# A retention layer that feeds a two-product block: another PSUM order in the dense product, stores on SyncE's queue, input scalings spread over a block, another opening

## The chip, the core and the metric

The kernel runs on one core of a Trainium2 chip. A core has a matrix engine (TensorE, PE in the profile), a vector engine (VectorE, DVE), a scalar engine (ScalarE, ACT), a general engine (GpSimd, POOL) and an engine that mostly issues transfers (SyncE, SP). Each works through its own list of instructions in order, and waits on semaphores. PE writes to PSUM, which the kernel uses as eight banks, each as large as a 128 x 512 tile of float32; DVE and ACT read PSUM and write SBUF. Transfers between memory and SBUF are done by 16 DMA engines, which take their work from queues; a queue belongs to the engine that issues to it. The metric is device time in microseconds (us) of one execution.

## What is computed

```python
def _attn_ref(q, k, v):                    # each (4, 8, 768, 64)
    gamma = 1.0 - 2.0 ** (-5.0 - np.arange(H))
    for t in range(S):
        state = gamma[None, :, None, None] * state + np.einsum('bhd,bhe->bhde', k[:, :, t], v[:, :, t])
        y[:, :, t] = scale * np.einsum('bhd,bhde->bhe', q[:, :, t], state)

def _moe_ref(x, w_in, w_out, alpha):       # x (3072, 512), w_in (512, 2048), w_out (2048, 512)
    h = x @ w_in
    g = np.maximum(h, 0.0) + alpha * np.minimum(h, 0.0)
    return g @ w_out
```

`x` is `y` with its heads side by side: 4 x 768 = 3072 tokens of 8 x 64 = 512 values. Inputs and output are float32 in memory; the products run in float16 and sum in float32.

## The kernel before

**Visits.** The retention is cut into 24 visits `w` of 256 time steps and 4 heads. A visit needs `load(w)`, three transfers of 256 KB (`ks`, `qs`, `vs`), all issued on SP's queue; `prep(w)`, which scales k and q by powers of gamma into one float16 tile `kdq` (k on DVE for the first eight visits and on POOL later, q on POOL) and converts v to `vx` (ACT for the first eight visits, POOL later); and the transposition of `kdq` into `kq`. For visits 0 to 7 PE does this (`turn(w)`: eight transposes into a PSUM tile `trb`, read by one ACT instruction); from visit 8 on a DMA does, issued on SP's queue in `prep`. Then PE computes the scores within 64 row pairs (`scores`, tile `sc`), the sums for the state (`state_sums`, tiles `st`), and, once DVE has masked the scores into `m2`, the values `y` (`within`, and `finish` with the rest of the `carried` part); ACT copies `y` to `xT`. `visit(w_old, w_new)` runs the end of one visit around the beginning of the next.

**Blocks.** Four visits give a block of 512 tokens, and there are six blocks. `ffn1(n)` computes 16 output tiles of 128 x 512, each as four matmuls; ACT then makes `hm` = relu(-h) and DVE `gt` = h + (1 - alpha) hm, in float16. `ffn2(n)` runs 64 matmuls into four PSUM tiles `ops`; each is copied to `os` by ACT and stored, 256 KB per store, by a transfer that ACT issues. Both are Python generators, one `yield` per matmul; `tick(gen, m)` emits m of them, so that the order of everything is written out by hand. While `ffn2(n)` runs, the visits of block n + 1 are ticked in; while `ffn1(n)` runs, `ahead()` emits `prep(w)` for a visit two blocks or so ahead, with its transposing DMA and the loads of visit w + 4 behind it. Block 0 and the first half of block 1 differ: the opening runs visits 0 to 3 alone, visits 4 to 7 run in and behind `ffn2(0)` (in four parts of 16 products) and in `ffn1_half(1, 0)`.

**PSUM.** Eight banks: tag `f` two single banks, `p` two single banks, `s` one tile of two banks, `y` one tile of two banks. `sc` and `trb` take `s`, `y` takes `y`, `st` takes `p`, `ops` takes `f`. `ffn1` takes its tiles from the class `Banks`, by a string: `f` and `p` ask for a bank, `s` or `y` for a two-bank tile, whose first half it gives out, and a capital letter gives the second half of the tile asked for last.

**DMA semaphores.** Transfers that SP and ACT issue share eight semaphores in turn (`DMAHW0` to `DMAHW7` in the orders below), so the issue of each waits for the transfer eight before it. The loads from visit 4 on are held (`held`) until a part of `w_out` has landed. Buffers: `ks`, `qs`, `vs`, `kdq`, `vx` and `kq` eight each, `os` six, `hm` three, `gt` two.

Among the lines of the profile: L140 loads, L157 scalings, L172 transposing DMA, L177 and L179 `vx`, L192 ACT's copy of `trb`, L213 scores, L270 and L292 `y`, L313 `xT`, L339 `gt`, L350 `hm`, L360 and L381 matmuls of `ffn1` and `ffn1_half`, L405 those of `ffn2`, L414 `os`, L418 the store.

## Time and profile before

| | before |
|---|---|
| median of 3 runs | 306.46 us (304.01 to 307.71) |
| profiled execution | 305.05 us, span of its instructions 303.3 us |
| busy: PE, DVE, ACT, POOL | 215.9, 134.1, 98.6, 57.9 us |
| mean granted clock of PE | 0.927 of full speed |
| chain that ended last | PE 57%, DVE 12%, ACT 9%, DMA 8% |
| output copies `os` and stores | 24 of each, stores on ACT's queue, 256 KB |
| transfers of SP's queue | 72 loads of 256 KB, 16 transposes |

Busy time is that of instructions that work; waiting, and the issuing of transfers, count as idle. An engine's waits are put down to the instruction of another engine, or the DMA, that ended last before the wait did. The chain follows the last instruction back to what released each. A granted clock of 1.0 is 2.4 GHz, 0.5 is 1.2 GHz. The DMA share is the mean busy share of the 16 DMA engines.

### The profile page before, as it was taken

To read this page: it belongs to the slowest core of one execution; us is meant where nothing else is said; L and a number is where in the kernel's file an instruction comes from. 1 tells how busy PE (TensorE), PEld (TensorE's weight loads), DVE (VectorE), ACT (ScalarE), POOL (GpSimd) and SP (SyncE) were. 2 spreads that over 40 slices of the span, in tenths; PEclk is the share of its full clock that TensorE was granted. 3 is DMA by queue.
4 is the path that set the end of the run, shared out by engine and by line. 5 is a ranking of instruction groups with operands and counts; after the bars stand their busy time and mean duration, and the time that the engine had idled before them with its cause. 6 is when DMAs were issued, how large, how long until landed. Compare 5 with 4: busy or idle time off the path is not lost.

```text
span 303.3 us, 5146 instructions
## 1 busy us (share of the span) xinstructions
PE 215.9 (71%) x2145; PEld 109.4 (36%) x2145; DVE 134.1 (44%) x242; ACT 98.6 (33%) x162; POOL 57.9 (19%) x68
## 2 busy tenths in 40 slices
PE   1659669946596877623769996699966999669900
PEld 0543324435484434201224542245422454224400
DVE  1754463433685733004356744655346652461000
ACT  3444341326462021104332353423434224351100
POOL 1740049800135634000006600000000000000000
PEclk9999999975999979775699999999999999999985
DMA  7999999619469999998000998001110011100111
GB/s 233 253 202 199 238 338 336 174 45 89 104 183 243 215 258 173 116 139 229 18 0 17 89 92 72 15 7 45 51 40 0 4 45 52 43 0 2 47 51 41
DMA packets 62599, 34.08 MB, mean 112 GB/s; under 512 B 18400, under 2 KB 59504, under 8 KB 62576
## 3 DMA queue, kind: packets, MB, share of 16 engines
q1 hardware_dynamic: 54912, 23.08, 43.5%
q0 software_dynamic: 4224, 4.19, 8.7%
q10 hardware_dynamic: 3440, 6.48, 5.9%
q8 instruction: 17, 0.28, 0.5%
q14 instruction: 6, 0.05, 0.1%
HBM read 27.45 MB, written 6.29 MB: 111 GB/s over the span
## 4 chain that ended last, share of the span: by engine, by line
PE 57%; DVE 12%; ACT 9%; DMA 8%; SPq 4%; ACTq 2%; issue 2%; POOL 2%; POOLq 0%
PE hps L360 24%; PE ops L405 24%; DVE gt L339 10%; ACT hm L350 5%; DMA kq<-kdq 4%; DMA ks<-in_k_dram 3%; PE sc L213 2%; ACTq L418 2%; PE hps L381 2%; SPq L140 2%; ACT kq L192 2%; DVE m L244 2%; PE y L270 2%; SPq L172 2%; DMA vs<-in_v_dram 1%
## 5 line engine op out<-in xcount | busy, mean ns | idle before, releaser
L339 DVE SCALAR_TENSOR_TENSOR gt<-hm,oma,hps 128x512 f16<-128x512 f32 (+1 forms) x112 | 73.1, 670 | 85.8 <-ACT hm L350 82.7
L360 PE MATMUL hps<-xT,win 128*128 128x512 f16 x320 | 79.8, 403 | 42.1 <-DVE gt L339 39.1
L405 PE MATMUL ops<-wout,gt 128*128 128x512 f16 x384 | 90.3, 385 | 2.4 <-ACT os L414 2.4
L350 ACT ACTIVATE hm<-hps 128x512 f32<-128x512 f32 x96 | 56.8, 597 | 81.2 <-PE hps L360 57.9
L360 PEld LDWEIGHTS <-win 128*128 128x128 f16 x320 | 32.6, 102 | 88.2 <-issue 56.8
L405 PEld LDWEIGHTS <-gt 128*128 128x128 f16 x384 | 35.8, 99 | 44.3 <-issue 4.9
L244 DVE TENSOR_TENSOR m<-sc,mi 128x1024 f16<-128x1024 f32 x24 | 29.4, 1223 | 14.4 <-PE sc L213 12.7
L157 POOL TENSOR_TENSOR kdq<-qs,tab 128x512 f16<-128x512 f32 x24 | 25.7, 1071 | 33.9 <-DMA qs<-in_q_dram 33.8
L313 ACT ACTIVATE xT<-y 128x512 f16<-128x512 f32 x24 | 14.3, 596 | 53.0 <-PE y L270 34.7
L157 POOL TENSOR_TENSOR kdq<-ks,tab 128x512 f16<-128x512 f32 x16 | 16.7, 1042 | 61.4 <-PE st L231 40.3
L414 ACT ACTIVATE os<-ops 128x512 f32<-128x512 f32 x24 | 14.3, 596 | 31.9 <-PE ops L405 30.7
L270 PE MATMUL y<-kq,tg 64*64 64x128 f16 x160 | 13.2, 256 | 11.3 <-ACT xT L313 7.7
L381 PE MATMUL hps<-xT,win 128*128 128x256 f16 x128 | 16.0, 281 | 4.5 <-DVE gt L339 3.3
L301 DVE MEMSET warm<- 1x1 f32 x24 | 1.4, 59 | 32.5 <-PE y L292 32.4
L258 DVE TENSOR_TENSOR tg<-ss,tab 128x128 f16<-128x128 f32 x32 | 14.8, 461 | 1.1
L381 PEld LDWEIGHTS <-win 128*128 128x128 f16 x128 | 12.4, 100 | 7.1 <-DVE gt L339 3.9
L179 POOL CAST vx<-vs 128x512 f16<-128x512 f32 x16 | 10.2, 639 | 22.4 <-PE y L292 11.3
L270 PEld LDWEIGHTS <-tg 64*64 64x64 f16 x160 | 6.3, 111 | 22.2 <-issue 15.4
L187 PE MATMUL trb<-mi,kdq 128*128 128x128 f16 x64 | 7.3, 279 | 9.5 <-DVE kdq L157 4.5
L213 PE MATMUL sc<-kq 64*64 64x128 f16 x384 | 11.3, 241 | 2.6 <-ACT kq L192 2.6
L192 ACT ACTIVATE kq<-trb 128x1024 f16<-128x1024 f16 x8 | 8.2, 1023 | 14.0 <-PE trb L187 13.4
L292 PE MATMUL y<-m,vx 64*64 64x128 f16 x384 | 11.8, 240 | 0.0
(21 smaller groups left out, 68.8 us busy)
## 6 DMA issues: line engine op xcount, KB each, us to landing
ks<-in_k_dram SPq DMA_DIRECT2D x24, 256.0 KB
qs<-in_q_dram SPq DMA_DIRECT2D x24, 256.0 KB
vs<-in_v_dram SPq DMA_DIRECT2D x24, 256.0 KB
out_dram<-os ACTq DMA_DIRECT2D x24, 256.0 KB
win<-in_moe_w_in_dram POOLq DMA_DIRECT2D x4, 512.0 KB, 7.7
wout<-in_moe_w_out_dram POOLq DMA_DIRECT2D x4, 512.0 KB, 15.1
kq<-kdq SPq DMA_TRANSPOSE x16
mi<-mi_const ACTq DMA_DIRECT2D x1, 128.0 KB
```

The source lines that it names most:

```text
L157: eng.tensor_tensor(out=kdq[:, kind].rearrange("p z r d -> p r z d"), in0=src.rearrange("p (r x) (a d) -> p r (x a) d", a=2, x=2), in1=tab ...
L213: nc.tensor.matmul(out=sc[half(c), at : at + 128], lhsT=kq[half(r), 2 * x + a, half(c)], rhs=kq[half(r), 4 + 2 * x : 6 + 2 * x, half(c)], ...
L244: nc.vector.tensor_tensor(out=m2.rearrange("p s a i -> p s (a i)"), in0=sc.rearrange("p (s n) -> p s n", n=256), in1=mask.unsqueeze(1).to_ ...
L258: nc.vector.tensor_tensor(out=tg, in0=stv, in1=decay, op=MULT)
L270: ins = nc.tensor.matmul(out=y[half(x), 512 * c + 128 * r : 512 * c + 128 * r + 128], lhsT=tgs[2 * u + c, g][half(r), x, :], rhs=kq[half(r ...
L313: nc.scalar.activation(out=xT[n][:, 2 * g : 2 * g + 2, TU * i : TU * i + TU].rearrange("p r (c i) -> p c r i", c=2), in_=y.rearrange("p (c ...
L339: nc.vector.scalar_tensor_tensor(out=gt[:, ft, lo:hi], in0=hm, scalar=oma_sb[:, ft : ft + 1], in1=hps, op0=MULT, op1=ADD,)
L350: nc.scalar.activation(out=hm, in_=hps, func=RELU, bias=0.0, scale=-1.0)
L360: nc.tensor.matmul(out=hps, lhsT=w_in_all[:, hp, 128 * ft : 128 * ft + 128], rhs=xT[n][:, hp, :], start=(hp == 0), stop=(hp == NP - 1),)
L381: nc.tensor.matmul(out=hps[:, TU * j : TU * j + TU], lhsT=w_in_all[:, hp, 128 * (f0 + j) : 128 * (f0 + j) + 128], rhs=xT[n][:, hp, lo:hi], ...
L405: nc.tensor.matmul(out=opss[tq], lhsT=gt[:, ft, 128 * tq : 128 * tq + 128], rhs=w_out_all[:, ft, :], start=(ft == 0), stop=(ft == NFT - 1),)
L414: nc.scalar.activation(out=os_sb, in_=opss[tq], func=COPY, bias=0.0, scale=1.0)
```

## The change

`ffn1` takes its tiles in the order `spyfSpYf`, and `Banks` remembers the first halves by tag, so that the second half can be asked for later. The stores are issued on `nc.sync`, SP's queue. In blocks 1 to 5 the four `ahead()` of a block, which were all in `ffn1`, stand two in `ffn1` (after 20 matmuls each) and two in `ffn2`. In the opening the loads come in another order, `turn` writes `trb` to a bank of tag `f` or `p`, products on a tile of ones (`busy`) are put in at four places, the state sums of visits 2 and 3 for the second chunk move into `ffn1(0)`, and visits 4 to 6 run inside an `ffn2(0)` that is in one piece, ahead of which stand the four `prep`. `visit` passes on a list of chunks (`cs`). Cut to its core:

```diff
+    ones = sbp.tile([128, 256], F16, tag="ones", name="ones")[:, 0:128]
-    def ps_s(name, dt=FP):
-        return ps(name, "s", 1024 if dt == FP else 2048, dt, 1)
     class Banks:
-            self.order, self.i, self.pair = order, 0, None
+            self.order, self.i, self.pairs = order, 0, {}
             if at in "sy":
-                self.pair = ps(name, at, 1024, FP, 1)
-                return self.pair[:, 0:512]
-            return self.pair[:, 512:1024]
+                self.pairs[at] = ps(name, at, 1024, FP, 1)
+                return self.pairs[at][:, 0:512]
+            return self.pairs[at.lower()][:, 512:1024]
-    def prep(w, opening=False, between=None):
+    def prep(w, opening=False, k_on=None):
-        scaled(nc.vector if opening else nc.gpsimd, 0, t["k"])
+        scaled(k_on or (nc.vector if opening else nc.gpsimd), 0, t["k"])
-        if between:
-            between()
+    def busy(m):
+        ips = ps("idle", "f")
+        for _ in range(m):
+            nc.tensor.matmul(out=ips[:, 0:128], lhsT=ones, rhs=ones, start=True, stop=True)
-    def turn(w):
+    def turn(w, tag, fill=0):
-        trb = ps_s("trb", F16)
+        trb = ps("trb", tag, 1024, F16)
         for i in range(8):
+            if i == 4 and fill:
+                busy(fill)
-    def ffn1(n, order="ffppsSyY"):
+    def ffn1(n, order="spyfSpYf"):
-                        nc.scalar.dma_start(
+                        nc.sync.dma_start(
+    nc.vector.memset(ones, 1.0)
-    for w in range(3):
-        load(w)
-    load(3, "kqv")
+    for w, which in ((0, "kqv"), (1, "kq"), (2, "kq"), (1, "v"), (3, "kq"), (2, "v"), (3, "v")):
+        load(w, which)
+    busy(34)
     prep(0, opening=True)
-    turn(0)
+    turn(0, "f", 12)
     prep(1, opening=True)
-    visit(None, 0)
+    busy(16)
+    scores(0)
...
+    prep(2, opening=True)
+    get_wi(0)
+    state(0)
...
+    turn(1, "f")
+    within(0)
+    scores(1)
+    state_sums(1)
+    finish(0)
+    masked(1)
+    prep(3, opening=True, k_on=nc.gpsimd)
+    state(1)
...
+    within(3)
+    busy(8)
+    finish(3)
     for w in range(WB, 3 * WB):
         load(w)
-    for _ in ffn1(0):
-        pass
-    gen = ffn2(0, parts=4, order="ffyY")
-    tick(gen, 44)
-    prep(4, opening=True)
-    turn(4)
...
+    gen = ffn1(0)
+    tick(gen, 32)
+    for w in (2, 3):
+        state_sums(w, (1,))
+        state(w, (1,))
     for _ in gen:
         pass
+    gen = ffn2(0)
+    for w in range(WB, 2 * WB):
+        prep(w, opening=True)
+    tick(gen, 30)
+    turn(4, "p")
+    tick(gen, 6)
+    visit(None, 4)
...
     gen = ffn1_half(1, 0, "ffpp")
     tick(gen, 8)
-    turn(7)
+    turn(7, "f")
...
-    gen = ffn1_half(1, 1, "ffppsSyY")
+    gen = ffn1_half(1, 1, "spyfSpYf")
     for n in range(1, NBLK):
         if n > 1:
             gen = ffn1(n)
-            for i in range(WB):
-                tick(gen, 14)
+            for i in range(2):
+                tick(gen, 20)
                 ahead()
...
             for i in range(1, WB):
-                tick(gen, 14)
+                tick(gen, 8)
+                if i == 2:
+                    ahead()
+                tick(gen, 6)
                 visit(w0 + i - 1, w0 + i)
-            tick(gen, 12)
+            tick(gen, 6)
+            ahead()
+            tick(gen, 6)
             within(w0 + WB - 1)
```

What this does to the lists of instructions shows at three places.

PE's list in `ffn1` of block 2, before (the matmuls alone, four for each tile; `hps` is an output tile, one number for both halves of a two-bank tile; a bracket says which engine's semaphore an instruction waits for):

```order
L360 MATMUL hps_1645<-xT2_1403,win_68 128x512
...
L360 MATMUL hps_1666<-xT2_1403,win_68 128x512
...
L360 MATMUL hps_1666<-xT2_1403,win_68 128x512 [waits DVE_49]
...
L360 MATMUL hps_1681<-xT2_1403,win_68 128x512 [waits PE_49]
...
L360 MATMUL hps_1681<-xT2_1403,win_68 128x512 [waits DVE_49]
```

The two halves of `hps_1666` come one right after the other, and the second waits for DVE; so it is with `hps_1681`. The same list after the change, in the same block:

```order
L377 MATMUL hps_1724<-xT2_1480,win_69 128x512 [waits Activation_49]
...
L377 MATMUL hps_1732<-xT2_1480,win_69 128x512
...
L377 MATMUL hps_1740<-xT2_1480,win_69 128x512 [waits PE_49]
...
L377 MATMUL hps_1748<-xT2_1480,win_69 128x512
...
L377 MATMUL hps_1724<-xT2_1480,win_69 128x512 [waits DVE_49]
...
L377 MATMUL hps_1776<-xT2_1480,win_69 128x512
...
L377 MATMUL hps_1740<-xT2_1480,win_69 128x512 [waits DVE_49]
...
L377 MATMUL hps_1791<-xT2_1480,win_69 128x512 [waits Activation_49]
```

Between the halves of `hps_1724` now stand three other tiles, as between those of `hps_1740`; the second half still has a wait for DVE.

SP's list where the transposes for block 3 begin (visits 12 and 13), before; `DMAHW` is one of the eight DMA semaphores:

```order
L172 DMA_TRANSPOSE kq12_1650<-kdq12_1648 128x8x128 [waits DMAHW3_49,PE_49,Pool_49]
L140 DMA ks16_1655<-in_k_dram 128x4x128 [waits DMAHW4_49,DVE_49]
L140 DMA qs16_1657<-in_q_dram 128x4x128 [waits DMAHW5_49]
L140 DMA vs16_1659<-in_v_dram 128x4x128 [waits DMAHW6_49,Activation_49]
L172 DMA_TRANSPOSE kq13_1691<-kdq13_1689 128x8x128 [waits DMAHW7_49,PE_49,Pool_49]
```

And after, at the same place:

```order
L435 DMA out_0_dram<-os_1416 2x64x512 [waits DMAHW3_49,Activation_49]
L171 DMA_TRANSPOSE kq12_1503<-kdq12_1501 128x8x128 [waits DMAHW4_49,PE_49,Pool_49]
L141 DMA ks16_1508<-in_k_dram 128x4x128 [waits DMAHW5_49,DVE_49]
L141 DMA qs16_1510<-in_q_dram 128x4x128 [waits DMAHW6_49]
L141 DMA vs16_1512<-in_v_dram 128x4x128 [waits DMAHW7_49]
L435 DMA out_0_dram<-os_1581 2x64x512 [waits DMAHW0_49,Activation_49]
L435 DMA out_0_dram<-os_1660 2x64x512 [waits DMAHW1_49,Activation_49]
L171 DMA_TRANSPOSE kq13_1668<-kdq13_1666 128x8x128 [waits DMAHW2_49,PE_49,Pool_49]
```

The stores, which ACT issued, stand between the loads and transposes, each with a wait for ACT's copy, and take their turns in the eight semaphores.

ACT's list in the opening, from its first conversion of v on (`vx`), before:

```order
L177 ACTIVATE vx0_100<-vs0_77 128x512 [waits DMAHW5_49]
L192 ACTIVATE kq0_101<-trb_105 128x1024 [waits PE_49]
L177 ACTIVATE vx1_116<-vs1_83 128x512 [waits DMAHW0_49]
L192 ACTIVATE kq1_117<-trb_167 128x1024 [waits PE_49]
L177 ACTIVATE vx2_178<-vs2_89 128x512 [waits DMAHW3_49]
L313 ACTIVATE xT0_241<-y_184 128x2x2x128 [waits PE_49]
L192 ACTIVATE kq2_179<-trb_251 128x1024 [waits PE_49]
```

And after:

```order
L176 ACTIVATE vx0_137<-vs0_79 128x512 [waits DMAHW5_49]
L201 ACTIVATE kq0_138<-trb_142 128x1024 [waits PE_49]
L176 ACTIVATE vx1_166<-vs1_89 128x512 [waits DMAHW2_49]
L176 ACTIVATE vx2_228<-vs2_95 128x512 [waits DMAHW5_49]
L201 ACTIVATE kq1_167<-trb_241 128x1024 [waits PE_49]
L329 ACTIVATE xT0_308<-y_251 128x2x2x128 [waits PE_49]
```

The conversion of v of visit 2 (`vx2`) now stands ahead of the copy of visit 1's transposes (`kq1`).

## Rows read from the trace of the kernel before

**Rows 1.** The page, section 1: busy us (share of the span), count of instructions.

```profile
PE 215.9 (71%) x2145; PEld 109.4 (36%) x2145; DVE 134.1 (44%) x242; ACT 98.6 (33%) x162; POOL 57.9 (19%) x68
```

**Rows 2.** Chain of waits, in order of time: start us, us, engine, what, count.

```profile
23.87 5.90 PE hps L360 x20
...
72.88 1.44 PE hps L381 x6
...
97.29 0.35 PE sc L213 x16
...
159.62 0.35 PE sc L213 x16
...
274.55 13.83 PE ops L405 x64
```

**Rows 3.** Windows: stretch, us, busy PE PEld DVE ACT POOL, PEclk, DMA share, GB/s.

```profile
121.20:159.00 37.80, 19.68 (x65) 7.38 (x64) 10.86 (x15) 9.72 (x17) 0.00 (x0) 0.73 0.64 101
...
177.20:197.50 20.30, 14.31 (x65) 6.17 (x64) 11.10 (x15) 9.48 (x16) 0.00 (x0) 1.00 0.64 53
197.50:215.70 18.20, 18.20 (x267) 9.00 (x266) 8.32 (x19) 4.70 (x9) 0.00 (x0) 1.00 0.09 31
```

**Rows 4.** Waits of PE (us, times, longest), in 177 to 216, then 45 to 97.

```profile
PE hps L360 <- DVE gt L339: 6.0, 4, 1.5
...
PE hps L381 <- DVE gt L339: 3.3, 2, 1.7
```

**Rows 5.** Timeline in a late ffn1: start us, us, engine line op, [idle before <-releaser].

```profile
182.98 1.89 PE L360 MATMUL hps<-xT,win 128*128 128x512 f16 x8 [1.47 <-DVE gt L339]
...
184.04 0.60 ACT L350 ACTIVATE hm<-hps 128x512 f32<-128x512 f32 x1 [1.89 <-PE hps L360]
184.67 0.75 DVE L339 SCALAR_TENSOR_TENSOR gt<-hm,oma,hps 128x512 f16<-128x512 f32 x1 [1.74 <-ACT hm L350]
```

**Rows 6.** Timeline in the middle, ACT and PE behind the stores of block 1.

```profile
137.12 2.73 ACT L350 ACTIVATE hm<-hps 128x512 f32<-128x512 f32 x5 [11.92 <-DMA kq<-kdq]
...
141.18 3.57 PE L360 MATMUL hps<-xT,win 128*128 128x512 f16 x8 [10.63 <-DVE gt L339]
```

**Rows 7.** Windows for the DMA engines (the last two columns).

```profile
34.00:36.00 2.00, 1.36 (x7) 0.65 (x7) 0.58 (x1) 0.30 (x1) 0.00 (x0) 1.00 0.94 243
44.00:46.00 2.00, 1.14 (x6) 0.54 (x6) 0.75 (x1) 0.10 (x2) 1.04 (x1) 1.00 1.15 345
...
166.00:186.00 20.00, 17.40 (x200) 8.12 (x199) 11.82 (x21) 7.60 (x13) 6.22 (x8) 1.00 1.27 90
...
214.00:224.00 10.00, 7.84 (x37) 3.43 (x37) 4.38 (x6) 5.30 (x9) 0.00 (x0) 1.00 0.13 51
280.00:302.00 22.00, 8.37 (x39) 3.63 (x37) 0.00 (x0) 1.79 (x3) 0.00 (x0) 0.80 0.13 48
```

**Rows 8.** SP's queue (start us, us to issue); then L172 (ns min/median/max, first to last).

```profile
33.09 0.37 SPq L140 DMA_DIRECT2D ks<-in_k_dram  x1
...
85.38 1.24 SPq L172 DMA_TRANSPOSE kq<-kdq  x1
...
104.36 2.92 SPq L172 DMA_TRANSPOSE kq<-kdq  x1
...
L172 SPq DMA_TRANSPOSE kq<-kdq x16: 1232/1658/6857, 53.3 to 175.9; - x16
```

**Rows 9.** Timeline of the opening.

```profile
11.94 0.64 PE L213 MATMUL sc<-kq 64*64 64x128 f16 x16 [0.44 <-ACT kq L192]
...
12.37 1.03 POOL L157 TENSOR_TENSOR kdq<-qs,tab 128x512 f16<-128x512 f32 x1 [0.34 <-DMA qs<-in_q_dram]
...
16.03 0.64 PE L213 MATMUL sc<-kq 64*64 64x128 f16 x16 [0.44 <-ACT kq L192]
```

**Rows 10.** Timeline of PE behind a stand, in ffn2 of block 1.

```profile
108.00 0.25 PE L270 MATMUL y<-kq,tg 64*64 64x128 f16 x4 [3.15 <-ACT xT L313]
...
108.90 4.78 PE L405 MATMUL ops<-wout,gt 128*128 128x512 f16 x14
```

More of the change, by code (lines that the diff above doesn't have):

```diff
@@ L180, in prep @@
         prepped[w] = (kdq, kq, vx)
-    def turn(w):
+    def busy(m):
+        ips = ps("idle", "f")
+        for _ in range(m):
+            nc.tensor.matmul(
+                out=ips[:, 0:128], lhsT=ones, rhs=ones, start=True, stop=True
+            )
+    def turn(w, tag, fill=0):
         kdq, kq, vx = prepped[w]
         flat = kdq.rearrange("p k z r d -> p (k z r d)")
-        trb = ps_s("trb", F16)
+        trb = ps("trb", tag, 1024, F16)
         for i in range(8):
+            if i == 4 and fill:
+                busy(fill)
             nc.tensor.transpose(
@@ L207, in scores @@
         kdq, kq, vx = prepped.pop(w)
-        sc = ps_s("sc")
+        sc = ps("sc", "s", 1024, FP, 1)
         for x in range(2):
@@ L219, in scores, with chunks, state_sums @@
                     )
-        live[w] = [kdq, kq, vx, sc, None]
-    def state_sums(w):
-        u, g, b, c3 = place(w)
-        kdq, kq, vx, sc, _ = live[w]
-        last = c3 == NUS - 1
-        sums = [ps(f"st{c}", "p") for c in range(1 if last else 2)]
+        raw[w] = kdq, vx
+        live[w] = [kdq, kq, vx, sc]
+    sums = {}
+    raw = {}
+    def chunks(w):
+        return (0,) if place(w)[3] == NUS - 1 else (0, 1)
+    def state_sums(w, cs=None):
+        kdq, vx = raw[w]
+        for c in cs or chunks(w):
+            sums[w, c] = ps(f"st{c}", "p")
         for x in range(2):
@@ L229, in state_sums @@
                 for c, r in DIAG:
-                    if c < len(sums):
+                    if c in (cs or chunks(w)):
                         nc.tensor.matmul(
-                            out=sums[c][half(r), 64 * x : 64 * x + 64],
+                            out=sums[w, c][half(r), 64 * x : 64 * x + 64],
                             lhsT=kdq[half(c), 0, 2 * x + a, r, :],
@@ L237, in state_sums, with masked @@
                         )
-        live[w][4] = sums
-    def after_scores(w):
-        u, g, b, c3 = place(w)
-        kdq, kq, vx, sc, sums = live[w]
+    def masked(w):
+        kdq, kq, vx, sc = live[w]
         m2 = sbp.tile([128, 4, 2, 128], F16, tag="m2", bufs=2, name="m2")
@@ L249, in after_scores, with state @@
         )
+        live[w][3] = m2
+    def state(w, cs=None):
+        u, g, b, c3 = place(w)
         decay = tab[:, 32 + 2 * g : 34 + 2 * g].unsqueeze(2).to_broadcast([128, 2, D])
-        for c, stp in enumerate(sums):
-            stv = stp[:, 0:128].rearrange("p (x e) -> p x e", e=D)
+        for c in cs or chunks(w):
+            stv = sums.pop((w, c))[:, 0:128].rearrange("p (x e) -> p x e", e=D)
             if c3 + c > 0:
@@ L284, in within @@
         u, g, b, c3 = place(w)
-        kdq, kq, vx, m2 = live[w]
+        vx, m2 = live[w][2:4]
         y = ps("y", "y", 1024, FP, 1)
@@ L323, in finish, with visit @@
         )
-    def visit(w_old, w_new):
+    def visit(w_old, w_new, cs=None):
         if w_old is not None:
@@ L329, in visit @@
             scores(w_new)
-            state_sums(w_new)
+            state_sums(w_new, cs)
         if w_old is not None:
@@ L333, in visit @@
         if w_new is not None:
-            after_scores(w_new)
+            masked(w_new)
+            state(w_new, cs)
     gts = {}
@@ L457 @@
     )
-    turn(1)
-    prep(2, opening=True, between=lambda: get_wi(0))
-    visit(0, 1)
-    turn(2)
-    prep(3, opening=True, between=lambda: get_wi(1))
-    visit(1, 2)
-    turn(3)
-    visit(2, 3)
-    get_wi(2)
-    get_wi(3)
+    turn(1, "f")
[6 more added lines that the diff above has]
+    state(1)
+    turn(2, "f")
+    within(1)
+    scores(2)
+    state_sums(2, (0,))
+    finish(1)
+    masked(2)
+    state(2, (0,))
+    turn(3, "f")
+    within(2)
+    scores(3)
+    state_sums(3, (0,))
+    finish(2)
+    masked(3)
+    state(3, (0,))
+    for i in range(1, 4):
+        get_wi(i)
     get_wo(0)
@@ L471 @@
     get_wo(3)
-    visit(3, None)
+    within(3)
+    busy(8)
+    finish(3)
     for w in range(WB, 3 * WB):
         load(w)
-    for _ in ffn1(0):
-        pass
-    gen = ffn2(0, parts=4, order="ffyY")
-    tick(gen, 44)
-    prep(4, opening=True)
-    turn(4)
-    tick(gen, 6)
-    prep(5, opening=True)
-    visit(None, 4)
-    tick(gen, 6)
-    turn(5)
+    gen = ffn1(0)
[3 more added lines that the diff above has]
+        state(w, (1,))
     for _ in gen:
         pass
-    prep(6, opening=True)
+    gen = ffn2(0)
[5 more added lines that the diff above has]
+    visit(None, 4)
+    tick(gen, 7)
+    turn(5, "p")
+    tick(gen, 6)
     visit(4, 5)
-    turn(6)
-    prep(7, opening=True)
+    tick(gen, 7)
+    turn(6, "p")
+    tick(gen, 6)
     visit(5, 6)
+    for _ in gen:
+        pass
     gen = ffn1_half(1, 0, "ffpp")
     tick(gen, 8)
-    turn(7)
+    turn(7, "f")
     tick(gen, 8)
@@ L533 @@
             for i in range(1, WB):
-                tick(gen, 14)
+                tick(gen, 8)
+                if i == 2:
+                    ahead()
+                tick(gen, 6)
                 visit(w0 + i - 1, w0 + i)
-            tick(gen, 12)
+            tick(gen, 6)
+            ahead()
+            tick(gen, 6)
             within(w0 + WB - 1)
```

5 lines of the change are left out of this document (3 added, 2 removed).

## The prediction

> **What bounds the kernel now.** I read the page first, then the chain of waits, the waits of TensorE (PE) by stretch, the timeline of one block, and last the windows for the DMA engines.
>
> PE is busy 71% of the span and no other engine comes near [rows 1]; the chain starts its long pieces at PE, and from 159.62 on nothing but PE, and short answers of ACT and DVE, is on it [rows 2]. So the late blocks are bound by PE's own order and what it waits for. A late block is ffn1 (20.3 us, PE busy 14.3) and then ffn2 with the visits of the next block (18.2 us, PE busy all of it) [rows 3]; the period is 38.5 us. In ffn1, PE waits four times for DVE's `gt`, 6.0 us in all [rows 4]. The timeline shows why: after five output tiles PE stands 1.5 us, until ACT (0.60) and DVE (0.75) have read the tile written last, then two tiles run (8 products), and it stands again [rows 5]. Both tiles lie in one two-bank PSUM tile, and the order `ffppsSyY` writes its halves one right after the other. Nobody else is late: DVE needs 0.75 us per tile and ACT 0.60, PE four products of 0.216, 0.87 [rows 2, 5].
>
> The middle is bound otherwise. From 121.2 to 159.0 PE is busy 19.7 of 37.8 us at a mean granted clock of 0.73 [rows 3]. ACT idles 11.92 us before 137.12, until a DMA is through: the store that it has to issue waits for a DMA semaphore. Behind it in ACT's queue stand the `hm` that PE's banks need, and PE stands 10.63 us [rows 6]. The DMA engines are the reason. While only stores run, the DMA share is 0.13, which is 2 of 16 engines, at 51 GB/s: 5.1 us for 256 KB. The last four stores keep that share up from 280 to 302, 5.5 us each [rows 7]. So a store occupies two engines alone, always the same two (otherwise four would overlap). Loads run at 345 GB/s, 0.76 us each [rows 7].
>
> **The change, part by part.** Durations are those of the profiled execution: span 303.3 us, 305.05 in all, so 1.75 around it; the median of the runs, 306.46, is 1.4 above.
>
> *Bank order `spyfSpYf`.* The halves are now written four tiles apart; a wait of a half is for the tile four back, which PE finished three tiles (2.6 us) before. Its readers need 0.60 + 0.75 plus some 0.1, 1.45 us: 1.1 us to spare [rows 5]. So 6.0 us go from each of the five full ffn1 (blocks 0, 2 to 5), and 3.3 us from the second half of block 1 [rows 4]. The cover is DVE's pace: 0.75 of work per 0.87; were that gone, 16 tiles at DVE's pace would still end with PE's. A late block becomes 14.3 + 18.2 = 32.5 us.
>
> *Stores from ACT's queue to SP's.* ACT no longer stands; the 10.63 us go, and the shorter stands of the same kind in block 1's ffn2. But SP's loads and transposes now stand in the same queue as the stores, and on the two engines that carry stores nothing passes them. I therefore add up what SP's order puts on those two engines. It begins, as before, with the loads that wait for the weights: 33.09 [rows 8], and full speed from about 35.0 (34 to 36 is at 243 GB/s) [rows 7]. Visits count from 0, four to a block, and ffn2 of a block holds the visits of the next. The last transpose with both loads and stores ahead and little time is that of visit 18, the third of block 4. Ahead of it and with it stand 54 loads x 0.76 = 41.0, 12 stores x 5.5 = 66.0, and 11 transposes.
>
> A transpose is the unknown. With no store in flight, six transposes with three loads each take 85.38 to 104.36, five steps of 3.8 us [rows 8]; less 2.28 for the loads that is 1.5. With stores in flight on the other queue four take 166 to 186, 5.0 each, DMA share 1.27 [rows 7]. Bounds: 1.2 (its shortest issue [rows 8]) and 5.0. I take 1.5: on one queue the two engines reach a transpose only after the store ahead is through, so it is the case without a store; the other engines can do their part meanwhile. Eleven make 16.5, and transpose 18 lands at 35.0 + 41.0 + 66.0 + 16.5 = 158.5. For visit 14 (42 loads, 8 stores, 7 transposes) it is 121.4.
>
> The Trainium skill (DMA: Bandwidth & Descriptors, section Queues, rings and completion order) says that a DMA engine takes turns between queues, packet by packet, and works off one queue in order. It speaks against this part: on ACT's own queue a store only halved the rate of those two engines, on SP's it holds everything behind it. The trace agrees that queues share (transposes stretch from 1.5 to 5.0 us beside stores, and still land). By that rule the sum above stands as it is.
>
> *Opening.* Before, a visit takes 4.1 us (scores at 11.94 and 16.03 [rows 9]); the transposes share two banks with the scores and wait until DVE has read those. They now have banks of their own. Yet v of visit 2 is now the eleventh load instead of the ninth, and its `vx` on ACT stands ahead of `kq` of visit 1. The eleventh load was there when POOL's last q scaling began at 12.37 [rows 9]; plus 0.62 for `vx` and 1.02 for `kq`, visit 1's scores start near 14.3 instead of 11.94. The three later steps then take 3.3 to 3.5 instead of 4.1. Sum: no gain, ffn1(0) at 23.8, plus or minus 1.5. The warm-up products (70 of 128 columns) run in PE's idle time. If they keep the clock at full, ffn1(0) saves the excess of its first 20 products, 5.90 against 20 x 0.216 = 4.33 [rows 2]; I count half.
>
> *Blocks 0 and 1.* ffn1(0): 21.9 (20.3 as later, plus that excess) - 6.0 + 0.3 for two state sums moved into it - 0.8 = 15.4, to 39.2. ffn2(0) in one piece: 64 products 13.9, three transposes 2.0, three visits 2.4, and 1.3 because ACT converts v of visits 4 to 7 ahead of the first output: 19.6, to 58.8. It needs all weights by 42, and they had landed when loads resumed (33.09) or shortly after. ffn1 of block 1 in halves: from 72.88, less 0.3 for two products ahead of it, to 97.29, less 0.6 of ffn2, 24.1 before; without the 3.3 of waits 20.8, to 79.6 instead of 96.7 [rows 2, 4].
>
> *Scalings spread.* POOL's work is the same; it moves code, not its limits, since POOL waits for loads. 0, covered by POOL's idle time (19% busy) [rows 1].
>
> **The sum.** PE alone gets from 79.6 to visit 18 with 18.2 + 32.5 + 14.3 + 9.0 (30 products and two visits): 153.6; the transpose lands at 158.5. So 4.9 us of standing, 0.3 of it at visit 14 (PE 121.1, DMA 121.4). After a stand of 3.15 us the clock was granted at half (1.2 GHz): 14 products took 4.78 us, against 14 x 0.216 = 3.02 [rows 2, 10]; I add 1.7. PE's own end: 79.6 + 18.2 + 3 x 32.5 + 14.3 + 28.8 (last ffn2 and its stores, 274.5 to 303.3 before [rows 2]) = 238.4. With 4.9 and 1.7: 245.0 of span, 246.8 in all: **247 us**. The tail stays as it was only if the older stores are through: by the same sum they are at 214.6 (34.1 of later entries up to transpose 23, then four stores), and the last block's first is ready at 245.0 - 28.8 + 3.5 + 0.6 = 220.3.
>
> So of the gain, PE's own waits give the late part, and what the opening or block 0 give or lose is swallowed, up to some 5 us, since the queue sets visit 18.
>
> **Rivals.**
> 1. *PE alone binds* (the queue is hidden): needs the sum of the two engines 4.9 us shorter, for instance stores at 5.1 instead of 5.5 (the rate of [rows 7]), 12 x 0.4. For it: that rate. Against: the four last stores. Time 238.4 + 1.75 = **240**.
> 2. *A transpose behind a store costs what it costs beside one*, 5.0: 11 x 3.5 = 38.5 more, **285**. For it: PE and queue are the same pieces. Against: on those engines the store has ended by then.
> 3. *The bank order does not do what it says* (the wait stays, since both halves are one tile). Waits stay before visit 18 (21.3, less the 4.9 and 1.7 that fall away) and after it (12.0): 247 + 26.7 = **274**. Against: the list of waits asks for the tile four back.
> 4. *Slower:* on SP's queue a transpose starts only with no store in flight and nothing passes it, so that it costs a store's time again, 5.5 + 1.5 or more. From 7.5 us each, 11 x 6.0 = 66, it decides: **313**. For it: the longest issue of a transpose was 6.86 us [rows 8]. Against: 3.8 us per step without stores. At 6.9 it would be no change.
>
> **Chances.** My forecast (241 to 264, a transpose between 1.2 and 3.0) 0.56; rival 1 0.17; rival 2 0.15; rival 3 0.04; no change 0.04; slower 0.04. The range goes from rival 1 with an opening and a clock that give 4 more, 236, to the forecast with stores at 6 us and transposes at 2.9 (6 + 15), 268; it leaves out 2 in 10. Over 2% is what a measurement here tells from no change; faster by that (under 300) are the first four: 0.92, same 0.04, slower 0.04.
>
> **What would show it.** Right: in ffn1 no PE wait for `gt`, 13.9 to 14.3 us per full ffn1; no idle time of ACT that ends with a DMA; DMA share at or above 0.13 without a gap from 35 to about 210; PE's longest stands before the scores of visits 14 and 18, released by the transposed tile `kq`, with a half clock after them; a last store 22 us after the first of its block. Wrong: PE waiting there for `gt` (bank order), transposes 5 us apart (rival 2), no stand before visit 18 (rival 1), or the first scores of block 2 before 75 or after 85.

## The result

The changed kernel takes 245.31 us (median of 4 runs, 243.66 to 246.41) where the kernel before takes 306.57: a ratio of 0.8006, with a 95% interval of 0.7938 to 0.8074. The prediction was 247 us, with a range of 236 to 268. The profiled execution took 245.44 us, with a span of 243.6; the granted clock was 0.925 on average, as before (0.927). Here and below, executions more than 1.5% slower than the fastest of their kernel are left out of medians and ratios.

The page of the changed kernel, section 1, answers to [rows 1]:

```profile
PE 212.6 (87%) x2215; PEld 112.3 (46%) x2215; DVE 130.5 (54%) x242; ACT 99.3 (41%) x162; POOL 58.4 (24%) x69
```

PE does nearly the same work (3 us less, in 70 more products) in a shorter span, and is busy 87% of it instead of 71%. The chain of waits of the changed kernel (start us, us, what, count), beside [rows 2]:

```profile
25.33 9.07 PE hps L377 x32
...
42.26 6.47 PE ops L422 x30
...
59.88 1.02 PE hps L398 x8
...
82.56 0.35 PE sc L222 x16
...
95.59 5.91 DMA ks<-in_k_dram
...
121.51 5.67 DMA kq<-kdq
...
139.37 5.56 SPq L171
...
148.94 8.87 DMA kq<-kdq
157.85 0.42 PE sc L222 x16
...
214.95 13.83 PE ops L422 x64
```

From 95.59 to 157.85 the chain runs through SP's queue: loads, POOL's scalings of what they brought, and transposes, with less than 1 us of PE. The last of these, a transposing DMA issued at 148.94, releases the scores of visit 18 at 157.85; behind that the chain is PE again. The windows of the changed kernel, to be read beside [rows 3] and [rows 7] (from the start of one block's ffn1 to that of the next, 3 us around its end, an ffn1, an ffn2 with visits, the tail):

```profile
100.06:132.88 32.82, 32.14 (x346) 15.20 (x345) 21.75 (x38) 14.23 (x24) 10.35 (x12) 1.00 1.10 155
131.00:134.00 3.00, 3.00 (x18) 1.25 (x17) 0.06 (x1) 1.25 (x3) 0.00 (x0) 1.00 0.13 42
...
132.88:146.69 13.81, 13.81 (x65) 6.27 (x64) 10.49 (x15) 9.55 (x16) 3.21 (x4) 1.00 0.89 116
...
183.10:201.10 18.00, 18.00 (x274) 8.95 (x272) 9.46 (x22) 4.70 (x8) 0.00 (x0) 1.00 0.22 61
...
228.50:242.50 14.00, 0.27 (x2) 0.00 (x0) 0.00 (x0) 0.60 (x1) 0.00 (x0) 0.58 0.13 49
```

An ffn1 is 13.8 us of nothing but PE, where it was 20.3. The stretch that took 37.8 us for one ffn1 in [rows 3] is gone: the same ffn1 and the ffn2 behind it now take 32.8 together. Asked in steps of 1 us, the DMA share does not fall under 0.12 from 35 to 211 us, but for 0.09 at 97, 0.06 at 132 and 0.06 at 188: the two engines that carry stores hardly rest, which the prediction's sum needs. The tail still shows two of sixteen DMA engines (share 0.13), 49 GB/s, 5.35 us for 256 KB. The place that the forecast named, in the timeline of PE:

```profile
132.88 13.98 PE L377 MATMUL hps<-xT,win 128*128 128x512 f16 x64
...
157.85 0.42 PE L222 MATMUL sc<-kq 64*64 64x128 f16 x16 [2.60 <-DMA kq<-kdq]
...
158.38 4.88 PE L422 MATMUL ops<-wout,gt 128*128 128x512 f16 x14
```

The 64 products of ffn1 are one run without a wait. PE stands 2.60 us before visit 18 for its transposed tile, and the 14 products behind the stand take 4.88 us instead of 3.02: the half clock, as in [rows 10].

### The profile page after: what moved, and what is told of

It is laid out like the page before. It is cut to its first block, busy times and chain, and to the rows that moved or that the text cites. A ratio compares the mean times of both kernels' runs of the same rounds, so it can differ in the third digit from the quotient of the medians.

```text
span 243.6 us, 5296 instructions
## 1 busy us (share of the span) xinstructions
PE 212.6 (87%) x2215; PEld 112.3 (46%) x2215; DVE 130.5 (54%) x242; ACT 99.3 (41%) x162; POOL 58.4 (24%) x69
## 4 chain that ended last, share of the span: by engine, by line
PE 57%; DMA 18%; SPq 9%; ACT 3%; DVE 3%; POOL 2%; issue 2%; POOLq 0%; ACTq 0%
PE ops L422 25%; PE hps L377 18%; PE hps L398 7%; DMA vs<-in_v_dram 6%; DMA kq<-kdq 6%; SPq L171 5%; DMA ks<-in_k_dram 5%; SPq L141 4%; PE sc L222 2%; POOL kdq L158 2%; PE y L286 2%; DMA qs<-in_q_dram 1%; PE y L308 1%; DVE m L257 1%; ACT kq L201 1%
## 5 line engine op out<-in xcount | busy, mean ns | idle before, releaser
L377 PE MATMUL hps<-xT,win 128*128 128x512 f16 x320 | 72.3, 387 | 0.3 <-DVE ss L272 0.3
L377 PEld LDWEIGHTS <-win 128*128 128x128 f16 x320 | 31.7, 100 | 39.4 <-issue 3.3
L257 DVE TENSOR_TENSOR m<-sc,mi 128x1024 f16<-128x1024 f32 x24 | 29.4, 1223 | 15.1 <-PE sc L222 13.5
L329 ACT ACTIVATE xT<-y 128x512 f16<-128x512 f32 x24 | 14.3, 597 | 50.8 <-PE y L286 49.8
L158 POOL TENSOR_TENSOR kdq<-ks,tab 128x512 f16<-128x512 f32 x17 | 17.8, 1049 | 56.6 <-PE hps L398 21.1
L431 ACT ACTIVATE os<-ops 128x512 f32<-128x512 f32 x24 | 14.3, 596 | 29.7 <-PE ops L422 29.6
L222 PE MATMUL sc<-kq 64*64 64x128 f16 x384 | 10.5, 230 | 7.7 <-ACT kq L201 4.4
L398 PEld LDWEIGHTS <-win 128*128 128x128 f16 x128 | 12.8, 102 | 4.8 <-issue 2.5
L275 DVE TENSOR_TENSOR tg<-ss,tab 128x128 f16<-128x128 f32 x32 | 12.1, 379 | 1.1
L222 PEld LDWEIGHTS <-kq 64*64 64x64 f16 x384 | 7.0, 112 | 10.9 <-ACT kq L201 5.4
L308 PE MATMUL y<-m,vx 64*64 64x128 f16 x384 | 11.2, 233 | 0.0
```

Of the source, the lines that this page charges most:

```text
L158: eng.tensor_tensor(out=kdq[:, kind].rearrange("p z r d -> p r z d"), in0=src.rearrange("p (r x) (a d) -> p r (x a) d", a=2, x=2), in1=tab ...
L222: nc.tensor.matmul(out=sc[half(c), at : at + 128], lhsT=kq[half(r), 2 * x + a, half(c)], rhs=kq[half(r), 4 + 2 * x : 6 + 2 * x, half(c)], ...
L257: nc.vector.tensor_tensor(out=m2.rearrange("p s a i -> p s (a i)"), in0=sc.rearrange("p (s n) -> p s n", n=256), in1=mask.unsqueeze(1).to_ ...
L308: last = nc.tensor.matmul(out=y[half(x), 512 * c + 128 * r : 512 * c + 128 * r + 128], lhsT=vx[half(c), 2 * r + x, a, :], rhs=m2[half(c), ...
L329: nc.scalar.activation(out=xT[n][:, 2 * g : 2 * g + 2, TU * i : TU * i + TU].rearrange("p r (c i) -> p c r i", c=2), in_=y.rearrange("p (c ...
L377: nc.tensor.matmul(out=hps, lhsT=w_in_all[:, hp, 128 * ft : 128 * ft + 128], rhs=xT[n][:, hp, :], start=(hp == 0), stop=(hp == NP - 1),)
```

## The experiments

My theory was the prediction's: three things set the time, the waits of PE inside ffn1 (bank order), the stands of ACT behind its stores (queue), and, once both are gone, the sum of what stands in SP's queue ahead of transpose 18, so that what the opening wins or loses is swallowed. Each ratio is to the kernel before on the same chip, where its median was 304.8 to 306.6 us; a difference between two runs is one of medians from different chips, so 1 us in it says little.

### Undoing the bank order

```diff
-    def ffn1(n, order="spyfSpYf"):
+    def ffn1(n, order="ffppsSyY"):
-    gen = ffn1_half(1, 1, "spyfSpYf")
+    gen = ffn1_half(1, 1, "ffppsSyY")
```

> The changed kernel with the old order of banks (ffppsSyY) in ffn1 and in the second half of block 1, all else as changed. My theory (the halves of a two-bank tile, written one after the other, cost PE 6.0 us in each of five ffn1 and 3.3 us in the half block, and of this what the queue would have cost anyway, the 2.6 us stand before the scores of visit 18 and some 2.5 us of half clock and smaller stands, is swallowed): 33.3 - 5.1 = 28 us more, 273 us (268 to 278), and again four waits of PE for gt of 1.5 us in a late ffn1. Rival (ffn1 is bound by DVE or ACT anyway, and the order only moves the wait): 245 to 250.

Measured: 275.69 us, ratio 0.8998 (0.8946 to 0.905). That is 30.4 us more than the changed kernel. The waits of PE in this run (us, times, longest):

```profile
PE hps L377 <- DVE gt L356: 30.0, 20, 1.5
...
PE hps L398 <- DVE gt L356: 3.3, 2, 1.7
```

Five ffn1 with 6.0 us each and the half block with 3.3 are back, just as in [rows 4], and the time is 2.7 us over the expected 273. No stand of PE for a transposed tile is left in this run: with PE this much slower the queue is not late. The order does what it says, and the rival (DVE or ACT binds anyway, 245 to 250) is out.

### Undoing the queue of the stores

```diff
-                        nc.sync.dma_start(
+                        nc.scalar.dma_start(
                             out=out[row : row + 128, :].rearrange("(p a) m -> a p m", a=2),
```

> The changed kernel with the stores back on ACT's queue, all else as changed. My theory (the stores' issue stops ACT, whose hm PE needs; on SP's queue it costs only the queue's own lateness): ACT stands again in the middle, PE loses the 10.6 us of one stand and some 5 of shorter ones, less the 5 us of standing and half clock at visit 18 that the queue costs now: 256 us (250 to 264), with transposes about 5 us long beside a store. Rival (a queue of their own lets the transposes pass the stores; ACT stood only because PE was late): faster than 245, down to 240, and no stand of PE before visit 18.

Measured: 274.4 us, ratio 0.8957 (0.8891 to 0.9023). Slower by 29.1 us: the direction was right and the size was not. The four stores of block 1 in ACT's queue (start us, us to issue), first in this run, with what PE does behind them:

```profile
103.92 0.52 ACTq L435 DMA_DIRECT2D out_dram<-os  x1
105.13 0.32 PE L286 MATMUL y<-kq,tg 64*64 64x128 f16 x4 [8.97 <-ACT xT L329]
115.15 0.52 ACTq L435 DMA_DIRECT2D out_dram<-os  x1
116.36 0.25 PE L286 MATMUL y<-kq,tg 64*64 64x128 f16 x4 [1.32 <-ACT xT L329]
121.23 0.52 ACTq L435 DMA_DIRECT2D out_dram<-os  x1
122.45 3.18 PE L377 MATMUL hps<-xT,win 128*128 128x512 f16 x14 [3.06 <-ACT xT L329]
133.67 0.52 ACTq L435 DMA_DIRECT2D out_dram<-os  x1
135.73 0.58 PE L377 MATMUL hps<-xT,win 128*128 128x512 f16 x1 [10.10 <-DVE gt L356]
```

and then in the kernel before:

```profile
106.78 0.52 ACTq L418 DMA_DIRECT2D out_dram<-os  x1
...
117.55 0.52 ACTq L418 DMA_DIRECT2D out_dram<-os  x1
...
118.77 0.25 PE L270 MATMUL y<-kq,tg 64*64 64x128 f16 x4 [1.56 <-ACT xT L313]
...
123.54 0.52 ACTq L418 DMA_DIRECT2D out_dram<-os  x1
...
124.76 5.79 PE L360 MATMUL hps<-xT,win 128*128 128x512 f16 x18 [2.96 <-ACT xT L313]
...
136.55 0.52 ACTq L418 DMA_DIRECT2D out_dram<-os  x1
```

They are issued at nearly the same times, though PE starts on this block's visits at 88.5 us in this run and at 97.2 in the kernel before. ACT's waits ahead of them end, as far as the trace tells, with a transfer of SP's queue (a `kq` or a `vs`), so it is the transfers that set these times, and not PE.

Where the size went wrong can be added up. The four stands of PE come to 23.4 us in this run (8.97, 1.32, 3.06, 10.10) and to 18.3 in the kernel before (3.15 [rows 10], 1.56, 2.96, 10.63 [rows 6]). Only the first grew, by 5.8 us, because PE came earlier and the store did not. My 10.6 and some 5 us were 2.7 short of the trace of before itself. They also left out the clock behind the stands: from ffn2 of block 1 to that of block 2 this run takes 60.6 us and the changed kernel 31.9, and this difference is 5.3 more than the stands. And 6.0 us are lost ahead of that, PE standing 3.15 and 2.36 us in ffn2 of block 0. With the 5.1 us at visits 14, 15 and 18 that this run is spared, this makes 29.6 us. The rival is out by the time, though no stand before visit 18 is left, as it said.

### The opening: no warm-up, and one conversion later

```diff
-    busy(34)
-    turn(0, "f", 12)
+    turn(0, "f")
-    busy(16)
-    busy(8)
```

> The changed kernel without the 70 products on ones, all else as changed. My theory (the clock that they win is lost again in the 3.64 us stand before the scores of visit 1, and whatever the opening loses is swallowed before visit 18): 245 us, within 1.5, and the scores of visit 18 at the same time, 157 to 158.5. Rival (the products keep the clock, and that counts to the end): 248 or more.

Measured: 244.66 us, ratio 0.7996 (0.7941 to 0.8051). No difference, as expected. The profiled execution, the shortest of its kernel (243.16 us), does not show the reason that I gave:

```profile
155.60 0.42 PE L222 MATMUL sc<-kq 64*64 64x128 f16 x16 [2.73 <-DMA kq<-kdq]
```

The scores of visit 18 came at 155.6 and not at 157 to 158.5, behind a stand as long as in the changed kernel, and the span is 241.4. So in this execution PE, the queue and the end are all some 2 us earlier, and nothing is swallowed. The sum in SP's queue dates visit 18 to some 2 us only; what made the queue earlier here is open.

The second run of this pair converts v of visit 2 behind the copy of visit 1's transposes (`prep` then returns the conversion, and `vx2()` emits it):

```diff
-    prep(2, opening=True)
+    vx2 = prep(2, opening=True, v_late=True)
...
     finish(0)
+    vx2()
     masked(1)
```

> The changed kernel with one step of the opening moved: the conversion of v of visit 2 on ACT stands behind the copy of visit 1's transposes and behind xT of visit 0. My theory: the 3.64 us stand of PE before the scores of visit 1 goes, ffn1 of block 0 starts near 21.7 instead of 25.3, perhaps earlier with a better clock, but the transpose of visit 18 still lands at 157 to 158 because the sum of the queue is the same, PE stands there 6 to 9 us instead of 2.6, and the time stays at 244 to 246. Rival (PE alone sets the time): 3.5 to 5 less, 240 to 242.

Measured: 244.83 us, ratio 0.8 (0.7949 to 0.8052). ffn1 of block 0 starts at 23.7 instead of 25.3 and its ffn2 at 39.8 instead of 42.1, and the end does not move. PE stands 5.8 us for transposed tiles instead of 3.3, most of it now one block earlier, before visit 14, and only 0.57 before visit 18:

```profile
125.61 0.64 PE L228 MATMUL sc<-kq 64*64 64x128 f16 x16 [3.60 <-DMA kq<-kdq]
...
159.61 0.42 PE L228 MATMUL sc<-kq 64*64 64x128 f16 x16 [0.57 <-DMA kq<-kdq]
```

I had put the stand at visit 18 and at 6 to 9 us, and its transpose at 157 to 158; it landed at 159.6. In this execution what the opening wins is swallowed, at the first place where the queue is behind. Over the profiled executions of the three kernels visit 18 is released at 155.6, 157.9 and 159.6, with the same entries in the queue; that the gain does not show at the end is a reading of the medians.

### All scalings of a block in ffn1

```diff
             gen = ffn1(n)
-            for i in range(2):
-                tick(gen, 20)
+            for i in range(WB):
+                tick(gen, 14)
                 ahead()
...
-                tick(gen, 8)
-                if i == 2:
-                    ahead()
-                tick(gen, 6)
+                tick(gen, 14)
...
-            tick(gen, 6)
-            ahead()
-            tick(gen, 6)
+            tick(gen, 12)
```

> The changed kernel with all four preparations of a block in ffn1 (after 14 products each), as before. My theory (only the order in SP's queue counts: all four stores of a block then stand ahead of the next block's four transposes, so visit 16 waits too, visit 18 has the same sum ahead of it, and visits 20 and on have two more stores): transpose 18 at 157 to 158 still, but stands of 2 to 3 us before visits 16 and 20: 247 us (245 to 250). Rival (no matter): 245, within 1.

Measured: 250.26 us, ratio 0.8204 (0.8129 to 0.8279), 5.0 us slower than the changed kernel by the medians and 6 by the ratios, more than I expected. SP's queue and PE in this run:

```profile
128.56 10.45 SPq L435 DMA_DIRECT2D out_dram<-os  x4
139.12 8.44 SPq L171 DMA_TRANSPOSE kq<-kdq  x1
```

```profile
116.97 0.42 PE L222 MATMUL sc<-kq 64*64 64x128 f16 x16 [2.30 <-DMA kq<-kdq]
...
154.00 0.42 PE L222 MATMUL sc<-kq 64*64 64x128 f16 x16 [3.47 <-DMA kq<-kdq]
...
189.94 0.42 PE L222 MATMUL sc<-kq 64*64 64x128 f16 x16 [2.37 <-DMA kq<-kdq]
```

All four stores of block 2 now stand ahead of transpose 16, which PE needs first in the next block; so PE stands before visits 12, 16 and 20, the first of each block, 8.1 us in three stands, and no longer before visit 18, where I had still expected the transpose at 157 to 158. POOL is not late: it has scaled k and q of visit 16 by 120 us, and the transpose is issued at 139.12. The places of `ahead()` are an order in SP's queue, and worth 5 to 6 us.

### Why a store is slow: its shape

The store's access pattern is 2 x 64 x 512. Two ways to give it more outer rows were run, and one of them together with the later conversion. First the columns of scores and `y` in the order of the tokens, so that a store is 128 rows in order:

```diff
-                        rhs=kq[half(r), 4 + 2 * x : 6 + 2 * x, half(c)],
+                        rhs=kq[half(r), 4 + 2 * x : 6 + 2 * x, half(c)].rearrange("k b i -> k i b"),
-                            out=out[row : row + 128, :].rearrange("(p a) m -> a p m", a=2),
+                            out=out[row : row + 128, :],
```

> The changed kernel, with the columns of the scores and of y in the order of the tokens (the moving operand of two groups of products read across, the mask to match), so that a store writes 128 rows in order instead of 2 groups of 64. My theory (a store occupies two DMA engines for 5.4 us because its outermost dimension is 2; with 128 rows it spreads over all 16 and takes about 1): no stand of PE for a transposed tile, minus 2.6 + 1.8 + 0.7 us, and the tail behind the last product, 14.2 us now, shrinks to about 3: 234 us (231 to 237). Rival (a store is slow for another reason, writing to memory): 245. Second rival (the product reads its moving operand slower across): scores and y longer than 0.22 us per group of 64 columns, and part of the gain lost.

Measured: 234.68 us, ratio 0.7703 (0.7651 to 0.7755). And each store cut in two:

```diff
+                        for a in range(2):
                             nc.sync.dma_start(
-                            out=out[row : row + 128, :].rearrange("(p a) m -> a p m", a=2),
-                            in_=os_sb,
+                                out=out[row : row + 128, :].rearrange("(p a) m -> a p m", a=2)[a],
+                                in_=os_sb[64 * a : 64 * a + 64],
```

> The changed kernel with each store cut into two, one for each group of 64 rows, nothing else. My theory: each half has an outermost dimension of 64 and spreads over the engines, so the time falls as with rows in order, but 48 issues of about 0.55 us stand in SP's queue instead of 24 and take turns at the eight semaphores: 235 us (232 to 239). Rival (a store is slow for another reason): 245 or more.

Measured: 229.57 us, ratio 0.751 (0.7455 to 0.7565). Windows of single stores near the end, first with rows in order, then in two halves (the last two columns: DMA share, GB/s):

```profile
221.90:222.70 0.80, 0.80 (x6) 0.36 (x4) 0.00 (x0) 0.00 (x0) 0.00 (x0) 1.00 0.85 328
```

```profile
214.70:216.10 1.40, 1.40 (x8) 0.67 (x7) 0.00 (x0) 0.00 (x0) 0.00 (x0) 1.00 0.80 186
...
223.30:228.00 4.70, 0.00 (x0) 0.00 (x0) 0.00 (x0) 0.60 (x1) 0.00 (x0) 0.88 0.24 56
```

0.8 and 1.4 us instead of 5.35, with a share of 0.80 to 0.85 instead of 0.13. In both no stand for a transposed tile is left, and the tail behind the last product is 4.7 us (two halves) instead of 14.8. The 15.7 us of the two halves are these two things: 10.1 of tail, and a last product that ends 5.5 us earlier, about as long as the stands and the half clock of the changed kernel (5.1). The Trainium skill (DMA: Bandwidth & Descriptors, section Why a DMA increments its semaphore by 16 and not by 1) says that the size of the slowest dimension of the patterns decides over how many engines a transfer runs; the windows agree, 2 rows with two of sixteen, 64 and 128 with nearly all.

Rows in order cost PE something that the two halves don't. The scores of one visit, with the moving operand read across, and in the changed kernel:

```profile
117.64 0.68 PE L222 MATMUL sc<-kq 64*64 64x128 f16 x16
```

```profile
114.39 0.42 PE L222 MATMUL sc<-kq 64*64 64x128 f16 x16
```

Over all visits the scores' busy time is 16.5 us instead of 10.5, and PE's in all 216.0 against 210.0 with the two halves: the second rival holds beside the theory, and it accounts for the 5 us by which two halves are better. What remains of the swallowing with short stores was seen by adding the later conversion of v of visit 2, the diff shown above, to the rows in order:

> Both: rows in order, and the conversion of v of visit 2 later. My theory: with the queue no longer late, the gain of the opening reaches the end: 3.6 us and some clock less than with rows in order alone, 229 us (227 to 232). Rival (the opening's gain is swallowed elsewhere): the same time as with rows in order alone, 234.

Measured: 232.7 us, ratio 0.7621 (0.7568 to 0.7673), 2.0 us less than rows in order alone. The same edit with the two halves (the two diffs above together):

> The changed kernel with each store cut into two halves of 64 rows, and the conversion of v of visit 2 later. My theory: with the queue no longer late, the opening's gain reaches the end; ffn2 of block 0 starts near 39.8 instead of 41.9, so 229.6 - 2.1 = 227.5 us (226 to 228.5). Rival (it is swallowed somewhere else): 229.6, within 0.5.

Measured: 228.01 us, ratio 0.7423 (0.7379 to 0.7468), 1.6 us less than the two halves alone, though the intervals overlap, as they do for the pair before. Both point the way of the theory (the opening's gain arrives), the first at 2.0 of the 5.7 us that I expected. In the profiled executions the gain of the opening itself is 3.5 and 1.0 us (ffn2 of block 0 starts at 40.6 instead of 44.1, and at 40.9 instead of 41.9), and the spans are 3.5 and 1.2 us shorter: there it arrives whole, and for the two halves it was smaller than the 2.1 us that I had taken.

And both edits with the four `busy` taken out:

> As the last one, without the 70 products on ones. My theory (the clock that they win falls back within some 7 us, in the opening's stands, and what follows is then longer at half clock than from a cold start): ffn2 of block 0 starts no later, near 39, and the time is 227 us (225.5 to 228). Rival (without the long stand the products keep the clock): 1 to 3 us more than with them.

Measured: 227.45 us, ratio 0.7445 (0.7405 to 0.7485): the same as with the products, as expected. In the profiled execution ffn2 of block 0 started at 38.9 instead of 40.9, as expected too, though it is the longest of its kernel (230.63 us).

### The shape alone, and the queue once the shape is right

The kernel before, with the store cut in two on ACT's queue and nothing else:

```diff
-                        nc.scalar.dma_start(
-                            out=out[row : row + 128, :].rearrange("(p a) m -> a p m", a=2),
-                            in_=os_sb,
+                        for a in range(2):
+                            nc.scalar.dma_start(
+                                out=out[row : row + 128, :].rearrange("(p a) m -> a p m", a=2)[a],
+                                in_=os_sb[64 * a : 64 * a + 64],
```

> The kernel before, with each store cut into two halves of 64 rows, both still on ACT's queue, nothing else. My theory (the stands of the middle and the slow tail both come from stores that occupy two DMA engines): ffn2 of block 1 and ffn1 of block 2 take 18.2 and 20.3 us, as in late blocks, instead of 23.9 and 37.8, and the tail behind the last product 3.5 instead of 14.2: 306 - 5.7 - 17.5 - 10.7 = 272 us (267 to 277), the four waits per ffn1 for gt unchanged. Rival (the stands come from the queue that the stores are issued on): 295, the tail alone gained.

Measured: four executions of 272.3, 277.4, 278.4 and 279.9 us. That is too wide for an interval; the shortest is the 272 that I expected, and the profiled one is the longest. In it the waits of PE for `gt` are as they were, but for one, and the stretch from the scores of block 2 to those of block 3, in this run and in the kernel before:

```profile
99.40:144.20 44.80, 35.70 (x341) 15.89 (x343) 22.59 (x37) 14.02 (x25) 10.51 (x12) 0.89 0.52 118
```

```profile
97.20:159.60 62.40, 39.58 (x341) 16.94 (x344) 22.43 (x37) 13.91 (x25) 10.99 (x13) 0.81 0.84 147
```

17.6 us of the 23.2 that I expected are gone there; one stand of 4.6 us stays, with half a clock behind it. What holds it I did not follow, and whether the execution of 272.3 us has it no trace tells. The rival (295) is out in all four. The change of shape alone is worth 26 to 33 us, about as much as either of the change's two large parts. The same five lines in the changed kernel, which puts its stores back on ACT's queue, but short:

> The changed kernel with each store cut into two halves, issued on ACT's queue. My theory: 48 issues of 0.52 us cost ACT 25 us of its idle time, and each still waits for the transfer eight before it, which may stand in SP's queue behind a transpose that waits for POOL, so ACT stands now and then: 233 us (230 to 240), not the 274 of whole stores on ACT. Rival (once the stores are short it no longer matters whose queue they are on): 229.6, within 0.5.

Measured: 238.72 us, ratio 0.7811 (0.7759 to 0.7863), within the range. Short stores on ACT's queue cost 9 us against SP's, where long ones cost 29; so the queue matters still, a third as much. ACT's issues, and the late `hm` behind them, show at one place of this run:

```profile
106.12 1.63 ACTq L436 DMA_DIRECT2D out_dram<-os  x2
107.85 2.07 ACT L367 ACTIVATE hm<-hps 128x512 f32<-128x512 f32 x4 [3.32 <-PE hps L377]
```

## Why the prediction was right, step by step

| step | predicted | measured |
|---|---|---|
| ffn1 of block 0 starts | 23.8 | 25.3 |
| it takes | 15.4 | 16.9 |
| ffn2 of block 0 with visits | 19.6 | 17.6 |
| ffn1 of block 1, two halves | 20.8 | 22.2 |
| ffn2 of block 1 starts | 79.6 | 82.1 |
| scores of visit 14 released | 121.4 | 122.7 |
| PE is at visit 18 | 153.6 | 155.25 |
| transpose 18 releases | 158.5 | 157.85 |
| stand, and half clock behind it | 4.9, 1.7 | 2.60, 1.86 |
| span | 245.0 | 243.6 |

**Bank order**: right, and to the size. No wait of PE for `gt` in ffn1 is left, an ffn1 takes 13.81 us (14.3 in the sum; just under the 13.9 to 14.3 named), and undoing it costs 30.4, of 33.3 by the waits.

**Stores on SP's queue, and the queue's sum**: right. From the scores of visit 14 to those of visit 18 it is 35.2 us; with 12 loads at 0.76 and four stores at 5.35 this leaves 4.7 for four transposes, 1.2 each, the lower bound, where 1.5 was taken. Stores were taken at 5.5. So the sum was 1.9 us too long for this block, visit 14 came 1.3 us later than by the sum, and the two nearly cancel. That 157.85 lies so near 158.5 is in part luck, and one execution: the queue ran between 155.6 and 159.6 in three. Rival 2 (5.0 per transpose) and the slower rival (7.5) are refuted by this, rival 3 by the waits. Rival 1 (PE alone) is refuted too, though only just: the stand and its half clock are 4.5 us, and 0.7 more stands before visits 14 and 15.

**Opening**: "I count half" of the clock's gain was wrong. The clock that the warm-up won fell back in the opening, around the stand before visit 1's scores, which the sum did name (14.3, measured 14.75). Windows of the opening of the changed kernel:

```profile
10.00:12.00 2.00, 0.47 (x18) 0.30 (x18) 1.38 (x6) 0.63 (x1) 2.00 (x2) 1.00 0.99 285
12.00:14.00 2.00, 0.00 (x0) 0.00 (x0) 0.00 (x0) 0.84 (x2) 1.98 (x3) 0.59 0.71 136
...
26.00:28.00 2.00, 2.00 (x6) 0.76 (x5) 0.18 (x1) 0.60 (x1) 0.00 (x0) 0.50 1.25 207
```

PE stands there for 3.64 us, the clock falls to half at about 12.4, and is half until 29.4, through the first quarter of ffn1. The long stand is not what it takes: with the conversion of v of visit 2 later, PE stands 1.24 us at most between the warm-up and the fall, and the clock is at half from 12.6 to 26.3. The warm-up won nothing: without it ffn1 of block 0 starts at 24.3 and takes 15.9 us, 1.0 less each. So the opening lost 1.5 us where I said no gain, and ffn1 another 1.5; ffn2 of block 0 gave 2.0 back and block 1's ffn1 took 1.4, which makes the 2.5 us by which PE comes late to block 1's ffn2. It did not matter to the end, and that was the forecast's last sentence on the sum: the medians of the runs without warm-up and with the earlier scores are within 0.7 us of the changed kernel's, while with short stores 1.6 to 2.0 us of the second arrive. It is shown by medians alone; in the profiled execution without warm-up 2.2 us did arrive.

**Scalings spread, costed at 0**: wrong by 5 to 6 us, the step that failed by most. The reason given, that they move POOL's code and not its limits, looked at POOL only. Each `ahead()` issues a transpose on SP's queue, and the spread puts two of four ahead of a block's late stores. (In block 1 all four stay in the second half of ffn1, and its ffn2 has two more; so two of the four of each later block come half a block earlier than before.) The sum for transpose 18 came out right all the same, since it was counted in the changed order; but as the price of the edit 0 was wrong. What it missed are the transfers that a moved step issues, and the queue that they are moved in.

**The sizes of the parts**: undone one at a time, the bank order is worth 30.4, the queue 29.1 and the places of the scalings 5 to 6 us, with the others there; they add up to some 65 against a whole of 61.3, so they overlap little. The warm-up is worth nothing here, and the earlier scores nothing as long as the stores are long; the opening as a whole was not undone.

**The signs named beforehand**: most are there, and three less clearly. The stand before visit 14 is 0.26 us, with 0.42 before visit 15 and no half clock behind them; PE's longest stand is the 3.64 us of the opening, and not one in the middle; and ACT still idles 10.2 us for loads of `vs` in its conversions, though never for a store. The last four stores run from 220.2 to 242.1, the 22 us named.

## What to carry to other kernels

Where one queue carries transfers that the critical engine waits for, write down what stands ahead of each of these and add it up; that sum, not the engine's own work, dated the stand before visit 18 to 1 us here (to 2 us over three executions), and gains of 2 us elsewhere did not show in the medians until it was cut. Look at a transfer's outermost dimension before moving it between queues: the two halves of a store in place of one, a few lines, brought 15.7 us on top of the change. A stand read from a trace is the price at that speed only: of four stands behind ACT's stores one went from 3.15 to 8.97 us when PE came earlier, and more than half of what was missed in their price was the half clock behind them, and stands elsewhere.

## What was not expected of the hardware

The two halves write every second row, the rows in order write one behind the other: 186 and 328 GB/s at nearly the same DMA share (0.80, 0.85). The halves are also two transfers of 64 partitions instead of one of 128, and no run tells the two apart. A moving operand read across (steps of 256 bytes) took the scores of a visit from 0.42 to 0.68 us; the Trainium skill (SBUF — State Buffer, section Door 1: The DMA port swizzle) says that reads that leave a 16-byte line each time are slower, and the row agrees.

In the run without warm-up the granted clock is shown as 1.00 throughout the opening, and yet eight transposes take 1.04 us there and 0.61 later; in the changed kernel they take the same 1.04 at a granted 0.50. The timeline of the run without warm-up:

```profile
18.47 1.04 PE L196 MATMUL trb<-mi,kdq 128*128 128x128 f16 x8
...
46.66 0.61 PE L196 MATMUL trb<-mi,kdq 128*128 128x128 f16 x8
```

So the granted clock of the profile tells of a fall, but not of a start at half speed; the durations do.
